# Order of issue in a fused retention and SwiGLU kernel: the later jobs' transposes two products behind a slot, their loads three

## The chip, the cores and the metric

The kernel runs on one NeuronCore of one Trainium2 chip. The metric is the device time of one execution in microseconds (us), as the median of three executions. A trace of one further execution gives the times of the single instructions; its span of 1141.5 us begins at the first instruction and ends with the last.

The engines of the core work side by side, each through its own instructions in the order in which the program wrote them: TensorE (PE in the profile) multiplies matrices, VectorE (DVE) and ScalarE (ACT) work on elements, GpSimd (POOL) does a little, and SyncE (SP) issues nearly all transfers between main memory (DRAM) and on-chip memory. "SPq" is SP's row of transfers. One row of issues serves the loads of queries, keys and values, the loads of weights and the stores of results.

## What is computed

```python
# retention, parallel form: 8 batches, 8 heads, 576 positions, 64 channels
scores = q @ k.T / sqrt(64)
ret    = scores * D            # D[i, j] = gamma_h ** (i - j) for i >= j, else 0
x      = (ret @ v)             # put together to 4608 tokens x 512 channels
# feed-forward with RMS norm and SwiGLU, 512 -> 1536 -> 512
xn  = x / sqrt(mean(x * x) + 1e-6) * rms_g
out = (silu(xn @ w_gate) * (xn @ w_val)) @ w_out
```

Queries, keys and values come as 32-bit floats. The weights come as 64-bit floats, and the kernel turns them into 32-bit floats itself: it loads both halves of each number as 32-bit words and takes sign, exponent and mantissa apart and together again with integer and float operations on VectorE and ScalarE.

## The kernel before

**Jobs.** Retention is cut into jobs of two heads each. Jobs 0 to 7 (batch 0 and a third of batch 1) are done at the start. Jobs 8 to 11 ("later jobs", the rest of batch 1) are done while the feed-forward of the first 768 tokens is already running. A job needs a load (`load_qk` and `load_kv`: 13 transfers), a turn (`prepare`: two transposes of 32 x 32 blocks on VectorE, and a scaling of the values on ScalarE) and a slot (`slot`: scores, states and sums of this job, and the values of the job before). The raw queries and keys have one buffer each, so a load waits in SP's row until the turn of the job before has read them.

```python
def load_qk(j):                       # 4 transfers for q, 4 for k; "raw" has one buffer
    ...
            t = raw.tile([P, S // SQ, SQ], F32, tag=nm + "raw", ...)
            ...
                    nc.sync.dma_start(out=t[...], in_=rows[i])            # L156
def load_kv(j):                       # 2 for k, 2 for v, 1 for the tail of v
    ...                                                                   # L224, L229
def prepare(j):                       # the turn
    for nm in ("q", "k"):
        ...
        nc.vector.transpose(out=t[:, t0:], in_=d.pop(nm + "raw")...)      # L272
    scale_v(j)                        # ACT, L285
def slot(j, rest=True):
    if rest and j > 0:
        values(j - 1)                 # PE, two PSUM banks av
    if j < len(jobs):
        scores(j)                     # PE
        states(j)                     # PE, one PSUM bank last
    ...
        weigh(j)                      # DVE
    if rest and j > 0:
        carried(j - 1)                # PE, then DVE empties av
    ...
        sums(j)                       # DVE, empties last
def prepare_next(j): prepare(j + 1)   # if there is such a job
def load_next(j): load_qk(j + 2); load_kv(j + 2)
def following(j):
    prepare_next(j)
    load_next(j)
```

**Chunks of weights.** There are 18 chunks of 1 MB as loaded: 0 to 11 for `w_gate` and `w_val`, 12 to 17 for `w_out`. Each is loaded into one of four spare places in buffers that aren't used yet. A place is free again when the last operation on the words of the chunk in it is done. The last six chunks use the places 1, 2, 3, 2, 3, 3, so that chunk 16 waits for 14 and chunk 17 for 16. The place 3 lies in the buffer of `w_gate`, the others in that of `w_out`.

```python
LATER = (1, 2, 3, 2, 3, 3)
def load_chunk(i, queue): ...
    queue.dma_start(out=dst, in_=src[rws, cols]...)      # L857
    there_at[i] = now + 3 if now else 0                  # not before 3 products from here
def exponent(i): ...                                     # DVE L874, then 3 x ACT L890 (act)
def mantissa(i):
    nc.vector.tensor_scalar(...);  yield                 # L901
    nc.vector.scalar_tensor_tensor(...);  yield          # L906, frees nothing yet
    act(chunk=i)                                         # the rest of the ACT operations
    nc.vector.scalar_tensor_tensor(...)                  # L911, last use of the words
    waits_at[spare(i)] = None                            # the place is free
def rounding():
    for i in range(len(chunks)):
        ...            # exponent(i), where it isn't done yet and the words may be there
                yield from mantissa(i)
                load_chunks(i + 5 if i else 0, nc.sync)
                yield
        ...            # exponent(i + 1) before or after that, where the words may be there
        join(i)                                          # L919
        yield
```

**The loop in which both meet.** The first 768 tokens go up through `w_gate` and `w_val` in 48 products, numbered by `now`. One product is 8 matmuls of 128 x 128 by 128 x 384 in the trace, and fills one of five PSUM banks that the whole kernel shares in rotation. Its result goes through `Silu` on ACT (L660) or is multiplied into that on DVE (L658), and that frees the bank. After each product come, in this order, what `later` has for this number, and two steps of the rounding.

```python
steps = rounding()
LATER_AT = (29, 33, 37, 41, 45)
def later(step):
    if step == LATER_AT[0] - 8:
        following(2 * NHP - 1)                 # turn 8, load 9
    elif step in LATER_AT:
        j = 2 * NHP + LATER_AT.index(step)
        if j < LATER_JOBS:                     # jobs 8 to 11
            slot(j, rest=(j > 2 * NHP))
            if j + 1 < LATER_JOBS:
                following(j)                   # turn j + 1, load j + 2
        else:
            values(j - 1)
            carried(j - 1)
...
for m, g in [(m, g) for g in range(NG) for m in range(2)]:
    for u in range(2):
        weights_to(4 * g + 2 * m + 1)
        for i, _ in enumerate(up_plain(u, m, g)):          # PE L652, then L660 or L658
            later(now)
            now += 1
            ...
            weights(2)
            act(1)
            if u and m and g == NG - 1:                    # products 44 to 47
                weights_to(len(chunks))
                next(made, None)                           # L690: blocks of w_out combined
            ...
```

After it the same tokens go down through `w_out` (`across(1)`, `across(0)`, PE L726), and then come ten rounds of 384 tokens each (PE L595 and L726) with the other jobs between them.

Of the kernel before, what the change touches and what calls it, by code (L numbers as in the profile page):

```python
# [22 lines left out]
def _decay_tables(H, D):  # L23

    pairs = _gamma(H).reshape(H // 2, 2).T
    rows = np.repeat(pairs, D, axis=0)
    pos = np.arange(L)
    p = np.concatenate([pos, pos])  # L30
    gq = rows[:, :, None] ** (pos + L) / np.sqrt(D)
    t = pairs.T[None] ** -p[:, None, None], rows**L, gq, np.roll(gq, D, axis=0)
    return [np.ascontiguousarray(x).astype(np.float32) for x in t]


def _causal_table():

    return np.ascontiguousarray(np.tile(np.triu(np.ones((L, L), np.float32)), (2, 1)))
# [3 lines left out]
def kernel(  # L42
# [15 lines left out]
    NHP = H // 2  # L58
# [29 lines left out]
    def bank(name):  # L88
        return banks.tile([P, 512], F32, tag="b", name=name)
# [46 lines left out]
    LATER_JOBS = 3 * NHP  # L136
# [9 lines left out]
    def load_qk(j):  # L146
        b, hp, c0, _ = jobs[j]
        for nm, src in (("q", q), ("k", k)):

            t = raw.tile([P, S // SQ, SQ], F32, tag=nm + "raw", name=f"{nm}raw_{j}")  # L150
            for e in range(2):
                rows = src[b, 2 * hp + e, c0 * L :]
                rows = rows.rearrange("(t b) (i a) -> i b t a", b=SQ, a=SQ)
                for i in range(D // SQ):
                    r = e * D + i * SQ
                    nc.sync.dma_start(out=t[r : r + SQ, c0 * L // SQ :], in_=rows[i])  # L156
            st[j][nm + "raw"] = t
# [58 lines left out]
    def load_kv(j):  # L216

        b, hp, *_ = jobs[j]
        i0, _ = tiles_of(j)
        for nm, src, bufs in (("k", k, 4), ("v", v, 3)):  # L220
            t = raw.tile([P, NFULL, 2, D], F32, tag=nm, name=f"{nm}_{j}", bufs=bufs)
            for e in range(2):
                rows = src[b, 2 * hp + e, i0 * P : NFULL * P]
                nc.sync.dma_start(  # L224
                    out=t[:, i0:, e], in_=rows.rearrange("(c p) d -> p c d", p=P)
                )
            st[j][nm] = t
        t = st[j]["vt"] = raw.tile([L, 2, D], F32, tag="vt", name=f"vt_{j}", bufs=3)
        nc.sync.dma_start(  # L229
            out=t, in_=v[b, 2 * hp : 2 * hp + 2, NFULL * P :].rearrange("e p d -> p e d")  # L230
        )
# [34 lines left out]
    def prepare(j):  # L266

        d = st[j]
        for nm in ("q", "k"):
            t = att.tile([P, S], F32, tag=nm + "T", name=f"{nm}T_{j}")  # L270
            t0 = jobs[j][2] * L
            nc.vector.transpose(  # L272
                out=t[:, t0:], in_=d.pop(nm + "raw")[:, t0 // SQ :].rearrange("p t a -> p (t a)")
            )
            d[nm + "T"] = t
        scale_v(j)
# [183 lines left out]
    def prepare_next(j):  # L460
        if j + 1 < len(jobs):
            prepare(j + 1)

    def load_next(j):
        if j + 2 < len(jobs):
            load_qk(j + 2)
            load_kv(j + 2)
# [4 lines that stand above are left out]
# [388 lines left out]
    def load_chunks(n, queue=nc.scalar):  # L860

        nonlocal n_loads
        while n_loads < min(n, len(chunks)) and waits_at.get(spare(n_loads)) is None:
            load_chunk(n_loads, queue)
            n_loads += 1
# [91 lines left out]
            yield  # L957

    steps = rounding()
    LATER_AT = (29, 33, 37, 41, 45)  # L960

    def weights(n):

# [13 lines left out]
    def start():  # L977

        nonlocal now
        h_of[0] = ffn.tile([P, NF, U], F32, tag="h", name="h_0")  # L980
        tables = list(zip((causal, gv, gc, gq, gx), (_causal_table(), *_decay_tables(H, D))))

        def table(i, queue):
            t, values_ = tables[i]
            src = nc.inline_tensor(values_, name=t.tensor.name + "_table")
            queue.dma_start(out=t, in_=src.ap())

        make_identity(nc, ident)
        nc.scalar.activation(out=tick, in_=mhalf[:1], func=AF.Silu)
        nc.vector.memset(ones, 1.0)  # L990
        warm = bank("warm")
        for _ in range(6):
            nc.tensor.matmul(warm[:, :P], lhsT=ones, rhs=ones, start=True, stop=True)
        first_places.update(find_places())
        load_chunks(1)
        for i in (1, 0, 2):
            table(i, nc.scalar)
        weights(3)
        for j in range(2 * NHP):
            load_first(j, {0: range(2), 1: range(2, H)}.get(j))  # L1000
            if j == 1:
                table(3, nc.sync)
            load_chunks((1, 1, 1, 1, 2, 2, 2, 3)[j], nc.sync)
        table(4, nc.sync)
        nc.sync.dma_start(out=rms_g, in_=moe_rms_g.rearrange("(c p) -> p c", p=P))
        load_chunks(4, nc.sync)
        turn(0)
        scale_v(0)
        act(3)
        squares = []  # L1010

        def later(step):

            if step == LATER_AT[0] - 8:
                following(2 * NHP - 1)
            elif step in LATER_AT:
                j = 2 * NHP + LATER_AT.index(step)
                if j < LATER_JOBS:
                    slot(j, rest=(j > 2 * NHP))
                    if j + 1 < LATER_JOBS:  # L1020
                        following(j)
                else:
                    values(j - 1)
                    carried(j - 1)

        for j in range(2 * NHP):
            slot(j)
            if j + 1 < 2 * NHP:
                turn(j + 1)
            if squares:  # L1030
                gather(*squares.pop())
            for i in ((1,), (2,), (3,), (4, 5), (6,), (7,), (), ())[j]:
                scale_v(i)
            if j:
                u, c = divmod(j - 1, NHP)
                squares.append((u, c, square(u, c)))
            act(1)
            if j == 5:
                norm_1(0)
            elif j == 6:  # L1040
                norm_2(0)
            weights((2, 0, 0, 1, 1, 1, 1, 0)[j])
            if j == 4:
                gather(*squares.pop())
            elif j == 5:
                diagonals(0)
            act(1)
        gather(*squares.pop())
        load_qk(2 * NHP)
        load_kv(2 * NHP)  # L1050
        made = combine_out()
        now = 0
# [3 lines that stand above are left out]
                for i, _ in enumerate(up_plain(u, m, g)):  # L1056
                    later(now)
                    now += 1
                    if not (u or m or g):
                        if i == 0:  # L1060
                            values(2 * NHP - 1)
                            carried(2 * NHP - 1)
                            gather(1, NHP - 1, square(1, NHP - 1))
                        elif i == 1:
                            norm_1(1)
                        elif i == 2:
                            diagonals(1)
                        elif i == 3:
                            norm_2(1)
                    weights(2)  # L1070
                    act(1)
                    if u and m and g == NG - 1:
                        weights_to(len(chunks))
                        next(made, None)
                    if i == 1:
                        weights_to(4 * g + 2 * m + 2)
        for _ in made:
            pass
        for blk, t in first_blocks.items():
            keep(blk, t)  # L1080
        rest = across(1)
        next(rest)
        following(LATER_JOBS - 1)
        for i, _ in enumerate(rest):
            if i == 1:
                norm_0(2)
                differences(0)
            elif i == 2:
                norm_1(2)
                diagonals(2)  # L1090
            elif i == 4:
                norm_2(2)
        rest = across(0)
        next(rest)
        combine(1)
        slot(LATER_JOBS, rest=False)
        following(LATER_JOBS)
        for _ in rest:
            pass
        combine(0)  # L1100
        slot(LATER_JOBS + 1)
        load_next(LATER_JOBS + 1)
        turns.append(LATER_JOBS + 1)
# [18 lines left out]
    with tc.manual_schedule():  # L1122
# [4 lines left out]
        for u in range(2, NU):  # L1127
# [11 lines left out]
            for i, _ in enumerate(rest):  # L1139
                if i == 0 and turns:  # L1140
                    prepare_next(turns.pop())
                if i == 2:
                    behind(u, 6)
                    at, n = SLOTS[u % 3]
# [33 lines left out]
```

## Time and profile before

| | |
|---|---|
| median of three executions | 1145.0 us (1144.41 to 1145.81) |
| execution with the trace | span 1141.5 us, mean granted TensorE clock 0.994 |
| busy share of the span | PE 98%, DVE 64%, ACT 23%, POOL 3% |
| the 48 products (L652) | first one at 47.4 us, last one at 191.6 us |
| loads of weight chunks (L857) | first 0.9 us (ACT's row), last 167.7 us (SP's row) |

The page of a profile gives totals over the whole span. For a change that moves a few instructions within a stretch of some 80 us, four other views are of more use: the list of waits (who stood still, for whom, how long in all, how often and the longest), the timeline of one engine (start, length, engine, line, operation), the chain that ended last, and the table of stretches (busy time of each engine, granted clock, DMA share and GB/s). A line such as L857 is one of kernel.py, printed above.

### The profile page before, as it was taken

How to read it: one execution, taken by the hardware profiler on the slowest of the kernel's cores; microseconds unless marked ns; L12 is line 12 of the kernel's file. 1: busy time of each engine (PE TensorE's matmuls, PEld its weight loads, DVE VectorE, ACT ScalarE, POOL GpSimd, SP SyncE). 2: the span in 40 equal slices, each digit the busy share in tenths (PEclk: the TensorE clock that was granted, in tenths of full speed). 3: DMA queues.
4: the chain of work that ended last, by engine and by line, in shares of the span. 5: the costliest groups of instructions: out<-in, count | busy, mean ns of one | idle time of the engine just before them, and what ended most of it. 6: DMA issues, size and time to landing. Idle time of an engine off the chain costs nothing.

```text
span 1141.5 us, 24777 instructions
## 1 busy us (share of the span) xinstructions
PE 1116.9 (98%) x10454; PEld 1041.7 (91%) x10454; DVE 733.0 (64%) x1452; ACT 258.0 (23%) x508; POOL 39.9 (3%) x68
## 2 busy tenths in 40 slices
PE   7899998999999999999999999999999999999998
PEld 6555655999999999999999999999999999999998
DVE  5888968746685685375767676466677566446352
ACT  5566532002211211211221121121121220120210
POOL 0100000380000000000000000000000000000000
PEclk8999999999999999999999999999999999999999
DMA  8744466335464465053454455305437503303304
GB/s 211 218 143 142 120 162 216 64 68 127 112 133 86 127 147 156 1 113 96 103 126 61 118 145 120 115 29 122 113 84 142 142 22 96 127 1 99 123 1 112
DMA packets 307040, 126.73 MB, mean 111 GB/s; under 512 B 284528, under 2 KB 289904, under 8 KB 306928
## 3 DMA queue, kind: packets, MB, share of 16 engines
q1 hardware_dynamic: 302640, 123.66, 42.8%
q8 instruction: 82, 1.34, 0.5%
q10 hardware_dynamic: 4288, 1.48, 0.5%
q14 instruction: 30, 0.25, 0.1%
HBM read 110.14 MB, written 14.94 MB: 110 GB/s over the span
## 4 chain that ended last, share of the span: by engine, by line
PE 89%; DVE 6%; DMA 1%; issue 1%; SPq 1%; ACT 1%; POOL 0%; DVEq 0%; POOLq 0%; ACTq 0%
PE w L595 13%; PE x L595 13%; PE z L595 13%; PE xo L726 8%; PE wo L726 8%; PE zo L726 8%; PE up L652 8%; PE y L595 6%; PE yo L726 4%; PE av L390 2%; PE s L307 1%; PE av L412 1%; PE s L329 1%; DVE sum L366 1%; DVE x L435 1%
## 5 line engine op out<-in xcount | busy, mean ns | idle before, releaser
L619 ACT COPY m<-x 128x384 f32<-128x384 f32 x60 | 28.7, 478 | 337.9 <-PE x L595 337.9
L726 PE MATMUL xo<-h,w_out 128*128 128x192 f32 x528 | 90.3, 328 | 0.0
L595 PE MATMUL w<-sums,w_val 128*128 128x192 f32 x480 | 88.6, 328 | 0.4
L595 PE MATMUL x<-x,w_val 128*128 128x192 f32 x480 | 88.8, 328 | 0.0
L595 PE MATMUL x<-x,w_gate 128*128 128x192 f32 x480 | 88.5, 328 | 0.0
L595 PE MATMUL w<-sums,w_gate 128*128 128x192 f32 x480 | 87.9, 326 | 0.0
L595 PE MATMUL z<-x,w_gate 128*128 128x192 f32 x480 | 87.8, 326 | 0.0
L595 PE MATMUL z<-x,w_val 128*128 128x192 f32 x480 | 87.8, 326 | 0.0
L726 PEld LDWEIGHTS xo<-h,w_out 128*128 128x128 f32 x528 | 85.9, 190 | 0.6
L726 PE MATMUL wo<-h,w_out 128*128 128x192 f32 x504 | 85.6, 326 | 0.4 <-DVE c_last L774 0.4
L602 DVE TENSOR_TENSOR u<-m,y 128x384 f32<-128x384 f32 x60 | 33.2, 553 | 79.1 <-PE y L595 79.1
L726 PEld LDWEIGHTS wo<-h,w_out 128*128 128x128 f32 x504 | 82.5, 190 | 0.7 <-DVE c_last L774 0.7
L595 PEld LDWEIGHTS w<-sums,w_val 128*128 128x128 f32 x480 | 79.2, 190 | 2.7 <-DVE c L602 2.7
L595 PEld LDWEIGHTS x<-x,w_val 128*128 128x128 f32 x480 | 79.2, 190 | 0.6
L595 PEld LDWEIGHTS x<-x,w_gate 128*128 128x128 f32 x480 | 79.3, 190 | 0.5
L595 PEld LDWEIGHTS z<-x,w_gate 128*128 128x128 f32 x480 | 79.7, 190 | 0.0
L595 PEld LDWEIGHTS z<-x,w_val 128*128 128x128 f32 x480 | 79.7, 190 | 0.0
L595 PEld LDWEIGHTS w<-sums,w_gate 128*128 128x128 f32 x480 | 79.5, 190 | 0.1
L602 DVE TENSOR_TENSOR h<-u,w 128x384 f32<-128x384 f32 x60 | 33.0, 551 | 69.5 <-PE w L595 69.5
L652 PE MATMUL up<-x,w_val 128*128 128x384 f32 x192 | 65.0, 497 | 5.6 <-DVE h L658 5.6
L614 ACT ACTIVATE h<-h 128x384 f32<-128x384 f32 x90 | 47.0, 523 | 88.7 <-DVE h L602 88.7
L652 PE MATMUL up<-x,w_gate 128*128 128x384 f32 x192 | 63.8, 489 | 2.0 <-DVE r L504 1.0
(189 smaller groups left out, 1774.6 us busy)
## 6 DMA issues: line engine op xcount, KB each, us to landing
w_out<-w_blocks SPq DMA_DIRECT2D x70, 768.0 KB, 4.9
out_dram<-o SPq DMA_DIRECT2D x364, 24.0 KB, 1.6
qraw<-in_q_dram SPq DMA_DIRECT2D x96, 72.0 KB, 2.6
kraw<-in_k_dram SPq DMA_DIRECT2D x96, 72.0 KB, 2.8
k<-in_k_dram SPq DMA_DIRECT2D x48, 128.0 KB, 2.8
v<-in_v_dram SPq DMA_DIRECT2D x48, 128.0 KB, 3.0
w_out<-in_moe_w_gate_dram SPq DMA_DIRECT2D x5, 1024.0 KB, 5.3
w_out<-in_moe_w_val_dram SPq DMA_DIRECT2D x3, 1024.0 KB, 5.2
```

The costliest lines, as they stand in the source:

```text
L307: nc.tensor.matmul(s[side(odd), e, i * L : i * L + L], lhsT=d["kT"][side(e), c * L : c * L + L], rhs=d["qT"][side(e), c * L : c * L + L], ...
L329: nc.tensor.matmul(o[side(e)], lhsT=d["k"][side(odd), i, e], rhs=d["v"][side(odd), i, e], start=True, stop=True,)
L366: nc.vector.scalar_tensor_tensor(out=d["sum"][c], in0=d["sum"][c - 1], scalar=gc[:, hp : hp + 1], in1=part, op0=ALU.mult, op1=ALU.add,)
L390: mm = nc.tensor.matmul(av[odd][column(j, odd, e), i * L : i * L + L], lhsT=d["v"][side(odd), i, e] if c < NC - 1 else d["vt"][:, e], rhs= ...
L412: mm = nc.tensor.matmul(av[odd][column(j, odd, e), i * L : i * L + L], lhsT=d["sum"][c - 1][side(e)], rhs=d["qT"][side(e), c * L : c * L + L],
L435: nc.vector.tensor_tensor(out=x[to, first - c0 // L :: 2], in0=av[odd][at, i * L : (i + n) * L].rearrange("p (c k) -> p c k", k=L), in1=g. ...
L595: nc.tensor.matmul(ps[:, i * HU : i * HU + HU], lhsT=w_up[m][:, 2 * blk + c, cut], rhs=t_of[u][blk][:, c], start=(start and i == c == 0), ...
L602: nc.vector.tensor_tensor(out=o, in0=a, in1=pairs_of(ps), op=ALU.add)
L614: nc.scalar.activation(out=o, in_=c, func=AF.Silu)
L619: nc.scalar.copy(out=s1, in_=pairs_of(x_))
L652: nc.tensor.matmul(ps[:, :U], lhsT=w_up[m][:, 4 * half + c, i * P : i * P + P], rhs=x_of[u][:, c], start=(c == 0), stop=(c == NHP - 1),)
L726: nc.tensor.matmul(ps[:, i * HU : i * HU + HU], lhsT=a[:, c, i * P : i * P + P], rhs=rhs[:, c], start=(start and i == c == 0), stop=False, ...
```

## The change

Slots, turns and loads of the later jobs are given other places among the 48 products. Slots come one product later. The turn of the next job no longer follows its slot directly but two products later, and the load of the job after that one more product later. In SP's row chunks of weights whose loads are written in between so stand ahead of these loads.

```diff
-    LATER_AT = (29, 33, 37, 41, 45)
+    LATER_AT = (30, 34, 38, 42, 46)
@@ def later(step):
-            if step == LATER_AT[0] - 8:
-                following(2 * NHP - 1)
-            elif step in LATER_AT:
+            for i, at in enumerate((LATER_AT[0] - 9,) + LATER_AT[:-2]):
+                if step == at + 2:
+                    prepare_next(2 * NHP - 1 + i)
+                elif step == at + 3:
+                    load_next(2 * NHP - 1 + i)
+            if step in LATER_AT:
                 j = 2 * NHP + LATER_AT.index(step)
                 if j < LATER_JOBS:
                     slot(j, rest=(j > 2 * NHP))
-                    if j + 1 < LATER_JOBS:
-                        following(j)
                 else:
                     values(j - 1)
                     carried(j - 1)
```

| after product | before | after the change |
|---|---|---|
| turn 8, load 9 | 21, 21 | 23, 24 |
| slot 8, turn 9, load 10 | 29, 29, 29 | 30, 32, 33 |
| slot 9, turn 10, load 11 | 33, 33, 33 | 34, 36, 37 |
| slot 10, turn 11, load 12 | 37, 37, 37 | 38, 40, 41 |
| slot 11 | 41 | 42 |
| values and carried part of job 11 | 45 | 46 |

No operation is added or taken away.

## The prediction

> **What bounds the kernel now.** I read the page first, then the list of waits, then the timelines of DVE and SP around the one wait that counts.
>
> ```profile
> span 1141.5 us, 24777 instructions
> PE 1116.9 (98%) x10454; PEld 1041.7 (91%) x10454; DVE 733.0 (64%) x1452; ACT 258.0 (23%) x508; POOL 39.9 (3%) x68
> ```
>
> PE is busy in 98% of the span, so a change of order can give back only idle time of PE. The list of waits says where PE stood still in the stretch that the change touches, and what stood behind it:
>
> ```profile
> DVE w_gate L874 <- DMA w_gate<-in_moe_w_out_dram: 10.2, 1, 10.2
> ...
> PE up L652 <- DVE h L658: 5.6, 1, 5.6
> ```
>
> PE waited once, 5.6 us, for a product to be read out of its bank (L658). DVE waited once, 10.2 us, for a chunk of weights. The timeline of DVE (start, length, engine, line) shows that they are one event:
>
> ```profile
> 156.75 0.75 DVE L342 SCALAR_TENSOR_TENSOR ret<-s,causal 128x256 f32<-128x256 f32 x2
> ...
> 160.00 0.57 DVE L272 STREAM_TRANSPOSE qT<-qraw 128x384 f32<-128x384 f32 x1
> 160.49 0.54 DVE L272 STREAM_TRANSPOSE kT<-kraw 128x384 f32<-128x384 f32 x1
> 160.95 1.18 DVE L911 SCALAR_TENSOR_TENSOR w_gate<-w_gate 128x1024 uint32<-128x1024 uint32 x1
> 162.17 1.23 DVE L919 SCALAR_TENSOR_TENSOR w_out<-w_out,w_gate 128x1024 f32<-128x1024 f32 x1
> 163.48 0.56 DVE L658 TENSOR_TENSOR h<-h,up 128x384 f32<-128x384 f32 x1
> 174.26 0.69 DVE L874 TENSOR_SCALAR w_gate<-w_gate 128x1024 uint32<-128x1024 uint32 x1 [10.22 <-DMA w_gate<-in_moe_w_out_dram]
> 174.87 0.69 DVE L901 TENSOR_SCALAR w_out<-w_gate 128x1024 uint32<-128x1024 uint32 x1
> 175.47 0.55 DVE L658 TENSOR_TENSOR h<-h,up 128x384 f32<-128x384 f32 x1
> ```
>
> L874 at 174.26 is the exponent of chunk 17. Behind it in DVE's row stands L658 of product 41, whose bank product 43 needs: five banks in rotation, and from 41 on they go to product 41, the two of slot 11's values, its `last`, product 42, and then to 43. PE resumes at 176.07. Why did chunk 17 come so late? SP's timeline:
>
> ```profile
> 160.60 1.96 SPq L156 DMA_DIRECT2D qraw<-in_q_dram  x4
> 162.65 2.06 SPq L156 DMA_DIRECT2D kraw<-in_k_dram  x4
> 164.76 1.05 SPq L224 DMA_DIRECT2D k<-in_k_dram  x2
> 165.92 0.99 SPq L224 DMA_DIRECT2D v<-in_v_dram  x2
> 167.02 0.61 SPq L229 DMA_DIRECT2D vt<-in_v_dram  x1
> 167.72 0.54 SPq L857 DMA_DIRECT2D w_gate<-in_moe_w_out_dram  x1
> ```
>
> Its place was free at 160.95 + 1.18 = 162.13, when L911 of chunk 16 ended. But load 12 stands ahead of it, starts when turn 11 has read the raw queries, and takes 7 us to issue. The chunk goes at 167.72 and lands at 174.2, 6.5 us after. One more line, from the table of stretches (busy times, then granted clock, DMA share, GB/s):
>
> ```profile
> 177.00:178.00 1.00, 1.00 (x3) 0.54 (x2) 0.95 (x4) 0.97 (x2) 0.00 (x0) 0.50 0.00 0
> ```
>
> After the stop PE runs at half its clock. The 8 matmuls of product 43 take 4.40 us on PE's timeline, those of 42 took 2.85: another 1.55 us. **The whole event costs 5.61 + 1.55 = 7.2 us.**
>
> **What the Trainium skill says.** "TensorE: Matmul & The Clock Gate", section "What's actually happening": the clock falls to half after an idle window of about 3.4 us and comes back after as long a busy one. The trace agrees: 5.6 us of idling, then 0.50 from about 175.5 to 178.9. So a stop well under 3.4 us should cost only itself. "DMA: Bandwidth & Descriptors", section "Anatomy of one DMA": "any semaphore wait happens on the issuing sequencer before dispatch". So a load whose buffer isn't free holds up all behind it; the chunk above, ready at 162.1 and gone at 167.7, shows it. "Perfetto Trace Analysis", section "Tensor Engine Instruction", has ACT and DVE as strict FIFO, PE with a little reordering; L658 at 175.47, whose product was there by about 166, shows it for DVE.
>
> **The change part by part.** From the code I listed what is written after each product. Loads of chunks 13, 14, 15, 16, 17 are written in the two rounding steps after products 22, 25, 30, 32, 37, and the change doesn't move them. It moves the loads of the jobs:
>
> - before: 12, load 9, 13, 14, load 10, 15, 16, load 11, load 12, 17
> - after: 12, 13, load 9, 14, 15, 16, load 10, load 11, 17, load 12
>
> So chunk 17 passes load 12, but load 11 now stands directly ahead of it. It won't go at once when its place is free.
>
> *PE.* A product is 2.63 us (four take 10.52, from 142.93 to 153.45), slot 8 0.98 us (129.75 to 130.73), a full slot 1.68 (141.25 to 142.93). Product 29 ends at 129.75 in both. After: product 36 ends at 129.75 + 7 x 2.63 + 0.98 + 1.68 = 150.8, product 38 at 156.1, slot 10 at 157.8, products 40, 41, 42 at 163.0, 165.7, 168.3, slot 11 at 170.0, product 43 at 172.6.
>
> *Chunk 16.* DVE work up to its load is the same as before (slot 8, turn 9, chunks 13 and 14), so it still goes at about 142.5, now with load 10 behind it. The one before took 8.3 us to land beside a load; I take that again: 150.8.
>
> *Turn 10 and load 11.* DVE has the exponent of 16 at about 150.9 (0.6), the join of 15 (1.2), then turn 10 from 152.7, with the queries read at 153.2. A load of 13 transfers took 8.0, 7.5 and 7.0 us to issue (133.56 to 141.55, 147.18 to 154.63, 160.60 to 167.63): 7.3 gives 160.5. The place of chunk 17 is free before that: behind turn 10 come 0.6 + 1.2 of mantissa and L911 with its ACT work, about 158. **Chunk 17 goes at 160.5** instead of 167.7. Landings of `w_out` chunks in the trace: 4.8, 5.5, 5.7, 5.9, 8.3, 6.5. I take 5.8, as load 11 is nearly through and nothing large is behind: it lands at 166.3, 8 us earlier.
>
> *DVE from there.* It has slot 10 (3.2 us) to about 161, L658 of product 40 to 163.7, turn 11 to 164.7, then waits some 1.6 us for the chunk instead of 10.2. Exponent and first mantissa to 167.4, L658 of 41 to 167.9, so product 43's bank is free well before 170. Three ACT operations of 1.15 from 166.9 end at 170.3; L911 to 171.5; L658 of product 42 at about 172.1. With slot 11 a product later, the rotation is 41, 42, values, values, `last`, 43, 44: product 44 needs 42's bank, at 172.6. It fits by half a microsecond, less than I can vouch for.
>
> *Behind.* DVE keeps that lag: slot 11 3.2, join 1.2, six L658 of 0.47, four L690 of 1.75, carried part of job 11 1.1, then L710 1.35 end near 189; `zo` of the first `across`, which reads L710's result, would begin 3.9 us after 184.6, at 188.5. Before, L710 ended at 195.9 and `zo` began at 196.13, as close. I put 0.3 to 0.5 us here.
>
> *Sum.* Back 7.2; given up again 0.3 to 0.5 at `zo` and on average 0.5 at product 44. Net 6.3. The 950 us behind are PE work with no dependence on this, and move up as a block. 1145.0 - 6.3 = 1138.7.
>
> **The rivals.** *The wait moves.* Load 11 still blocks the row; a landing of 8.3 instead of 5.8 puts L658 of 42 at 174.6 and stops product 44 for 2 us, at full clock afterwards. For it: the landing of chunk 16. Time 1140 to 1141. *A full gain:* all margins hold, also the 0.26 and 0.32 us PE waits nearby go: 1137.2. *Turns come too late:* a turn has two products (5.3 us) ahead of its slot, a load three (7.9) ahead of its turn while its issue alone takes 7.3; if values of job 11 came late at ACT, slots would stop PE and DVE would become the bound. Against it: load 11 is through at 160.5, its last transfer lands 2.3 later, slot 11 comes at 168.3. It would make 1143 to 1148. *Hidden anyway:* it isn't, since PE has no slack behind.
>
> **Range and chances.** Full gain and moved wait with run-to-run spread (0.7 us each way) give 1137.0 to 1141.0. 2% is 22.9 us, three times what the event costs, so faster by 2% is out of reach; slower by 2% would need a new stop of over 20 us.
>
> **What would show it.** In the profile after: the chunk load of SP (L857, last) near 160.5 and ahead of load 12; DVE's wait for it 1 to 3 us instead of 10.2; no granted clock of 0.50 between 165 and 192; PE's wait for L658 gone or under 2 us, and if there, ahead of product 44; product 47 ending near 185. Wrong, if load 11's issue starts much later than 153, if chunk 17 lands after 169, or if a slot waits for a transpose or a scaled value.

## The result, and the profile after

The changed kernel takes 1136.39 us (median of four executions, 1135.36 to 1138.52) where the kernel before took 1144.7 beside it: a ratio of 0.9928, with a 95% interval of 0.9911 to 0.9946. The prediction was 1138.7 with a range of 1137.0 to 1141.0, so the gain came out larger than the range allowed.

The page of the traced execution, its span and busy shares:

```profile
span 1135.3 us, 24783 instructions
PE 1116.6 (98%) x10454; PEld 1042.3 (92%) x10454; DVE 732.7 (65%) x1452; ACT 258.6 (23%) x508; POOL 40.9 (4%) x68
```

Work is the same on every engine. What changed is waiting. The list of waits of PE between 60 and 215 us, that is nearly all of the 48 products and the first part of the way down, is now

```profile
PE up L652 <- DVE x L564: 0.7, 1, 0.7
PE av L412 <- POOL tick L401: 0.3, 1, 0.3
```

Both were there before. The 5.6 us for L658 are gone, and so is a wait of 0.3 for L660 ahead of product 38 (more on that one below). No granted clock of one half is left between the products. SP's timeline shows load 11, then chunk 17, then load 12:

```profile
154.52 1.90 SPq L156 DMA_DIRECT2D qraw<-in_q_dram  x4
156.51 1.95 SPq L156 DMA_DIRECT2D kraw<-in_k_dram  x4
158.51 1.01 SPq L224 DMA_DIRECT2D k<-in_k_dram  x2
159.63 0.95 SPq L224 DMA_DIRECT2D v<-in_v_dram  x2
160.69 1.60 SPq L229 DMA_DIRECT2D vt<-in_v_dram  x1
162.39 0.54 SPq L857 DMA_DIRECT2D w_gate<-in_moe_w_out_dram  x1
165.99 1.95 SPq L156 DMA_DIRECT2D qraw<-in_q_dram  x4
```

and DVE's timeline the short wait for the chunk and the results of products 41 and 42 behind it:

```profile
165.89 0.54 DVE L272 STREAM_TRANSPOSE kT<-kraw 128x384 f32<-128x384 f32 x1
167.64 0.69 DVE L874 TENSOR_SCALAR w_gate<-w_gate 128x1024 uint32<-128x1024 uint32 x1 [1.21 <-DMA w_gate<-in_moe_w_out_dram]
...
168.85 0.55 DVE L658 TENSOR_TENSOR h<-h,up 128x384 f32<-128x384 f32 x1
...
171.91 1.23 DVE L911 SCALAR_TENSOR_TENSOR w_gate<-w_gate 128x1024 uint32<-128x1024 uint32 x1 [1.38 <-ACT w_gate L890]
173.06 0.55 DVE L658 TENSOR_TENSOR h<-h,up 128x384 f32<-128x384 f32 x1
```

The wait of DVE is 1.21 us instead of 10.22, because the transpose work of turn 11 and slot 10 now lies ahead of it and the chunk comes earlier. L658 of product 42 ends at 173.6, and PE starts product 44 near 174.3 without stopping.

**One measure for all runs.** The start of the kernel differs from execution to execution: the first product of `w_val` (product 8) begins between 72.8 and 74.9 us in the eleven traces of this study, in kernels that are the same up to there. So I measure the stretch on PE from the start of product 8 to the first matmul of `xo` in the way down, read from PE's timeline. Before it takes 192.24 - 72.90 = 119.34 us, after 186.29 - 74.36 = 111.93. **The stretch gives 7.41 us.** PE's timeline before, and then after the change:

```profile
72.90 20.80 PE L652 MATMUL up<-x,w_val 128*128 128x384 f32 x64
...
167.62 2.85 PE L652 MATMUL up<-x,w_val 128*128 128x384 f32 x8
176.07 9.56 PE L652 MATMUL up<-x,w_val 128*128 128x384 f32 x24 [5.61 <-DVE h L658]
...
192.24 4.06 PE L726 MATMUL xo<-w_val,w_out 128*128 128x192 f32 x24
```
```profile
74.36 20.80 PE L652 MATMUL up<-x,w_val 128*128 128x384 f32 x64
...
171.66 10.59 PE L652 MATMUL up<-x,w_val 128*128 128x384 f32 x32
...
186.29 4.06 PE L726 MATMUL xo<-w_val,w_out 128*128 128x192 f32 x24
```

From the start of the first of four products to the first matmul behind them it is 185.56 - 167.62 = 17.94 us with the stop and 182.17 - 171.66 = 10.51 us without. So the event alone costs 7.43 us: 5.61 of stop, 1.55 of slow clock, and some 0.27 because a stop also breaks the overlap of one product with the next (one product alone shows 2.85 us, but products in a row start 2.63 us apart). The small wait for L660 has no part in the 7.41: slot 10 takes 0.29 us less without it (1.70 for 1.99), and slot 9 0.28 us more (1.96 for 1.68).

| kernel | stretch, us | median beside before, us | ratio (95%) |
|---|---|---|---|
| before | 119.34 | | 1 |
| the change | 111.93 | 1136.39 : 1144.7 | 0.9928 (0.9911 to 0.9946) |
| e1, the change again | 111.93 | 1136.85 : 1144.09 | 0.9940 (0.9926 to 0.9953) |
| e2, load 12 alone moved | 111.92 | 1135.48 : 1144.09 | 0.9925 (0.9909 to 0.9940) |
| e3, slots alone moved | 113.95 | 1138.33 : 1144.09 | 0.9950 (0.9936 to 0.9965) |
| e4, last third undone | 120.71 | 1145.11 : 1144.09 | 1.0011 (1.0004 to 1.0017) |
| e5, chunk 17 from ACT's row | 111.95 | 1135.59 : 1143.69 | 0.9928 (0.9913 to 0.9942) |
| e6, chunk 17 inside load 12 | 113.64 | 1137.75 : 1143.69 | 0.9945 (0.9931 to 0.9960) |
| e7, first use written later | 111.92, then 4.8 lost at `zo` | 1140.03 : 1143.69 | 0.9964 (0.9949 to 0.9978) |
| e8, slots, and load 10 later | 117.62 | 1141.3 : 1143.69 | 0.9978 (0.9969 to 0.9988) |
| e9, turns and loads alone | 113.45 | 1139.27 : 1143.69 | 0.9957 (0.9943 to 0.9971) |

The differences of the medians follow the stretches to within 1.5 us; the intervals are as wide. Where less than that matters, the stretch decides.

### The profile page after: what moved, and what is told of

Its sections match the earlier page's. It is cut to its first block, busy times and chain, and to the rows that moved or that the text cites. A ratio compares the mean times of both kernels' runs of the same rounds, so it can differ in the third digit from the quotient of the medians.

```text
span 1135.3 us, 24783 instructions
## 1 busy us (share of the span) xinstructions
PE 1116.6 (98%) x10454; PEld 1042.3 (92%) x10454; DVE 732.7 (65%) x1452; ACT 258.6 (23%) x508; POOL 40.9 (4%) x68
## 4 chain that ended last, share of the span: by engine, by line
PE 96%; DVE 1%; DMA 1%; issue 1%; ACT 1%; SPq 0%; POOL 0%; POOLq 0%; ACTq 0%
PE x L595 14%; PE w L595 14%; PE z L595 14%; PE up L652 11%; PE xo L726 8%; PE wo L726 8%; PE zo L726 8%; PE y L595 7%; PE yo L726 4%; PE av L390 2%; PE av L412 2%; PE s L307 2%; PE s L329 1%; PE ms L513 1%; DMA first_sums<-in_v_dram 0%
```

## The experiments

The theory: chunk 17 was held up by what stands ahead of it in SP's row, its first use then held up DVE's row, and results behind that held up PE. The rivals: the room that later turns and slots give DVE is what counts; memory bandwidth is what counts; the change gives something outside of the stretch.

**e1: the change again,** unchanged.

> The changed kernel once more, to size its gain. Traces so far: from the end of product 29 to the first matmul of the down part the kernel before took 62.5 us and the changed one 55.1, so the stretch gave 7.4 (5.6 of stop, 1.55 of half clock, 0.26 of a small wait). The medians differ by 8.3. If the stretch is all there is (theory: the row of SP), the gain over five rounds is 7.4, and what is over comes from the start, whose length differs from run to run. Rival: the change gives something elsewhere too, and the gain is again above 8.

The stretch is again 111.93 us, and the ratio 0.9940. The medians differ by 7.2, not 8.3. Nothing outside of the stretch is needed to account for it. The traces say the same: from the first matmul of `xo` to the end of the span it is 949.3 us before, 949.0 after the change and 949.3 in e1.

**e2: only load 12 behind chunk 17,** in the kernel before.

```diff
             elif step in LATER_AT: ...
-                    if j + 1 < LATER_JOBS:
-                        following(j)
+                    if j + 1 < LATER_JOBS:
+                        prepare_next(j)
+                        if j < LATER_JOBS - 2:
+                            load_next(j)
+            elif step == LATER_AT[2] + 1:
+                load_next(LATER_JOBS - 2)
```

> The kernel before with one move only: the load of job 12 is written one product later, so that chunk 17 stands ahead of it. Slots and turns stay. Theory of the row: chunk 17 goes when its place is free, at 162.2, lands near 168, DVE waits about 4 us for it instead of 10.2, PE does not stop at all, the gain is the whole 7.4. Rival (later turns and slots give DVE room, the loads are by the way): gain under 2.

Chunk 17 went at 163.21, or 162.2 after the later start is taken off, DVE waited 3.7 us for it, and PE didn't stop for a result of DVE. Its small wait of before is still there:

```profile
PE up L652 <- ACT w_val L660: 0.3, 1, 0.3
```

One load written one product later gives all that the change gives: slots, turns and the other three loads needn't move.

**e3: only the slots one product later,** turn and load still right behind each.

```diff
-    LATER_AT = (29, 33, 37, 41, 45)
+    LATER_AT = (30, 34, 38, 42, 46)
-            if step == LATER_AT[0] - 8:
+            if step == LATER_AT[0] - 9:
```

> The kernel before with slots 8 to 11 one product later and turn and load still right behind each slot. That alone puts chunk 17 between load 11 and load 12 in the row of SP. Theory of the row: chunk 17 goes when its place is free, about 159 to 162, no stop of PE, gain 7.4, so two products more for the turns and three for the loads add nothing. Rival (it is the distance of turns and loads that counts): a stop of some us remains, gain 2 to 5.

The stop for chunk 17 is gone, as its load again passes load 12, but another one is there. The waits of PE and of DVE:

```profile
PE up L652 <- ACT h L660: 2.1, 1, 2.1
...
DVE w_gate L874 <- DMA w_out<-in_moe_w_out_dram: 4.5, 1, 4.5
```

This is chunk 15. It still stood behind load 10, which came later with its slot, and went at 144.09 instead of 141.65 (1.2 of that is the later start of this execution). DVE waited for it, an ACT operation of that chunk waited for DVE, and a result of PE (L660) stood behind that in ACT's row. The later issue explains 1.3 of DVE's 4.5 us. The rest fits the slot's own move: in the kernel before, DVE's work for slot 9 and turn 10 (143.3 to 147.6) stands ahead of this chunk's exponent and fills the time, and with the slot one product later it stands behind. I had looked only at chunk 17 and expected the whole 7.4; the stretch gives 5.4.

**e4: the last third of the change undone:** slot 10, turn 11 and load 12 again after product 37.

```diff
-    LATER_AT = (30, 34, 38, 42, 46)
+    LATER_AT = (30, 34, 37, 42, 46)
-            for i, at in enumerate((LATER_AT[0] - 9,) + LATER_AT[:-2]):
+            for i, at in enumerate((LATER_AT[0] - 9,) + LATER_AT[:2]):
...
                     slot(j, rest=(j > 2 * NHP))
+                    if j == LATER_JOBS - 2:
+                        following(j)
```

> The changed kernel with slot 10, turn 11 and load 12 put back behind product 37; everything else stays changed. Chunk 17 then stands behind load 11 and load 12, both late. Theory of the row: load 11 goes from 154 to 162, load 12 to 169, chunk 17 near 169.5, landing near 176; PE stops 6 to 8 us and falls to half clock; the whole gain is lost, 1144 to 1147. Rival (later turns and slots): most of the moves are still there, so half of the gain or more stays, under 1141.

SP's timeline gives chunk 17 at 169.27. PE's timeline shows the stop and what comes after:

```profile
177.31 13.57 PE L652 MATMUL up<-x,w_val 128*128 128x384 f32 x32 [5.68 <-DVE h L658]
```

Four products take 13.57 us where they take 10.59 at full clock. The whole gain is lost with two thirds of the moves still in place. The rival of "more room for DVE" falls. But SP's row isn't all of this delay. The place of chunk 17 came free only at 166.9, when L911 of chunk 16 ended: that had waited 4.6 us for ACT, and ACT had waited 5.4 us for the values of load 11, behind which turn 11 now stands directly. Load 12 held the chunk up for the last 2.4 us.

**e5: chunk 17 issued from ACT's row,** nothing else.

```diff
-                    load_chunks(i + 5 if i else 0, nc.sync)
+                    load_chunks(i + 5 if i else 0, nc.scalar if n_loads == 17 else nc.sync)
```

> The kernel before with one change: the transfer of chunk 17 is issued from ACT instead of SP; no order is changed. Theory of the row: ACT has no load ahead of it, so the chunk goes at 162.2 when its place is free and lands near 168.5, PE does not stop, gain 7.4 less what ACT's own row loses by waiting from 159 to 162 (under 0.5). Rival (the memory side is the limit, the chunk shares the bandwidth with load 12 in any case): landing stays after 172, gain under 3.

ACT's timeline, then one line of DVE's:

```profile
162.21 0.40 ACTq L857 DMA_DIRECT2D w_gate<-in_moe_w_out_dram  x1
162.65 0.87 ACT L660 ACTIVATE w_val<-up 128x384 f32<-128x384 f32 x2 [3.60 <-DVE w_gate L911]
```
```profile
167.91 0.69 DVE L874 TENSOR_SCALAR w_gate<-w_gate 128x1024 uint32<-128x1024 uint32 x1 [3.82 <-DMA w_gate<-in_moe_w_out_dram]
```

The transfer waited 3.6 us in ACT's row for its place and went at 162.21, while load 12 was being issued by SP from 160.64 on. The stretch is 111.95 us. With both on the way at once the chunk was there for DVE at 167.9: memory bandwidth isn't what held it up. Load 12 took 9.5 us to issue here instead of 7.0, which cost PE nothing.

**e6: chunk 17 in the middle of load 12.**

```diff
-                        following(j)
+                        prepare_next(j)
+                        if j < LATER_JOBS - 2: load_next(j)
+                        else: load_qk(j + 2)
+            elif step == LATER_AT[2] + 1:
+                load_kv(LATER_JOBS)
```

> The kernel before with chunk 17 in the middle of load 12: the 8 transfers of queries and keys ahead of it, the 5 of keys by rows and values behind. It goes near 164.7 and lands near 170.5 to 171. Product 41's result is then read out near 172.2, so PE stops for 1.5 to 2.5 us. If the slow clock comes only after an idle stretch of some 3.4 us, that stop costs itself alone and the gain is 5 to 6 us, with no granted clock of 0.50 in the stretch; if any stop brings the half clock, 1.5 less: 3.5 to 4.5.

PE's timeline:

```profile
172.27 8.01 PE L652 MATMUL up<-x,w_val 128*128 128x384 f32 x24 [1.44 <-DVE h L658]
```

The chunk went at 165.17. PE stopped for 1.44 us, and the three products after it took 8.01 us, full clock. The stop is 4.2 us shorter than before, and the stretch 5.7 shorter: the rest is the slow clock that didn't come, as expected (the 3.4 us are those of the page that the prediction names).

**e7: only the first use of chunk 17 written later,** no transfer moved.

```diff
-        there_at[i] = now + 3 if now else 0
+        there_at[i] = now + (6 if i == 17 else 3) if now else 0
```

> The kernel before with no transfer moved: only the first DVE operation on chunk 17 (exponent) is written three products later, behind the results of products 41, 42 and 43. Chunk 17 still lands at 174. If what stops PE is the wait inside DVE's row, ahead of results that PE's banks need, PE does not stop and the gain is 7 or more with SP's row as it was. If chunk 17 itself is needed by then, the stop comes a little later and most of the 7 stays lost.

PE no longer stopped at product 43, although the chunk was issued at 169.48 (168.0 on the scale of the kernel before) and first used at 175.77. So it was the wait inside DVE's row that stopped PE. But DVE's own chain got late. Its timeline, then PE's (`issue` means that the profile shows nothing that PE waited for):

```profile
191.77 1.35 DVE L710 TENSOR_TENSOR t<-w_val 128x1152 f32<-128x1152 f32 x1
```
```profile
186.30 4.06 PE L726 MATMUL xo<-w_val,w_out 128*128 128x192 f32 x24
193.23 5.82 PE L726 MATMUL zo<-t,w_gate 128*128 128x192 f32 x24 [2.86 <-issue]
```

`zo` normally begins 3.90 us after `xo`; here it was 6.93, and it took 5.82 instead of 4.06 at half clock: 3.03 + 1.76 = 4.8 us given back. The late join and combination of `w_out` (L690) pushed L710, which `zo` reads: it ended at 193.12, and `zo` began 0.11 us later. Half of my expectation held; I hadn't followed the chunk past product 47.

**e8: the slots of e3, and load 10 behind chunks 15 and 16.** Turn 10 stays right behind slot 9, after product 34.

```diff
 (beside the lines of e3)
+            elif step == LATER_AT[0] + 3:
+                load_next(2 * NHP)
...
-                        following(j)
+                        prepare_next(j)
+                        if j > 2 * NHP:
+                            load_next(j)
```

> Slots one product later with turn and load right behind each, and one more move: load 10 is written after product 33, behind chunks 15 and 16. With the slots alone chunk 15 went only at 144.1, behind load 10, DVE waited 4.5 us for it, and PE 2.1 us for a result that ACT held up. If that chunk behind that load made the whole stop, it is gone here: chunk 15 goes near 139, the stretch takes 111.9 us as in the changed kernel, gain 7.4. If the slots' new place stops PE by itself, some 2 us stay lost.

Chunk 15 went at 137.57, and its stop was gone. But load 10 went at 142.75, and its turn came one product behind. Waits of PE, then ACT's timeline:

```profile
PE last L329 <- ACT w_val L660: 1.8, 1, 1.8
PE av L390 <- ACT h L660: 1.2, 1, 1.2
PE up L652 <- ACT w_val L660: 0.7, 1, 0.7
```
```profile
153.26 0.45 ACT L285 ACTIVATE v<-v,gv 128x192 f32<-128x192 f32 x1 [7.54 <-DMA v<-in_v_dram]
```

ACT waited 7.5 us for the values that the turn scales, with results of PE behind it. The stretch is 5.7 us longer than that of the change, an outcome that I hadn't named. A load that goes later needs its turn to go later too, as e4 shows as well; the change moves the turns by two products.

**e9: turns and loads as changed, slots as before.**

```diff
-    LATER_AT = (30, 34, 38, 42, 46)
+    LATER_AT = (29, 33, 37, 41, 45)
-            for i, at in enumerate((LATER_AT[0] - 9,) + LATER_AT[:-2]):
+            for i, at in enumerate((21, 30, 34, 38)):
```

> The changed kernel with the slots (and the last values) back at products 29, 33, 37, 41, 45; turns and loads stay where the change has them, after 23 and 24, 32 and 33, 36 and 37, 40 and 41. The order in SP's row is that of the changed kernel. Theory of the row: gain 7.4, stretch of 111.9 us, so the slots' move gives nothing. Rival (a turn one product ahead of its slot is too near): PE waits up to 1 us in slots 10 and 11, gain 6 to 7.

```profile
PE s L307 <- DVE kT L272: 1.6, 1, 1.6
```

The order of SP's row is that of the change, but a turn now lies one product ahead of its slot, and in slot 10 PE waited 1.6 us for a transpose. The stretch is 1.5 us longer than with the slots moved as well. The rival held here, with a longer wait than it named: with the turns moved, slots at their old places cost something. The distance alone isn't the reason. In e4 turn 10 lies one product ahead of slot 10 too, and PE didn't wait: there the transposes ended 80.6 us after the start of product 8, here 82.7 us after it, behind a wait of DVE of 1.95 us for ACT.

## Why the prediction was wrong

**What bounds, and why: right.** One event, and its chain (load 12 ahead of chunk 17, L874 ahead of L658, bank of product 41, PE). Its cost was a quarter of a microsecond too small: I had 7.2, from start to start it is 7.43, as the overlap with the next product is lost as well. The two small waits that I had put into the full gain gave nothing: the one of 0.26 us went, but slot 9 got as much longer, and the one of 0.32 us stayed. One reading was loose. The passage that I quoted on semaphore waits describes transfers that GpSimd issues; for SP's row it is the trace that shows such a wait, 5.9 us ahead of load 12. And this wait was over at 160.60. From 162.1, when the chunk's place was free, SP was busy issuing load 12.

**The new order and its times: right.** The traced execution begins product 8 1.46 us later than that of before; taken off, chunk 17 went at 160.9 (I had 160.5), was used at 166.2 (166.3), and L658 of product 42 ended at 172.15 (172.1). In e1 SP issued it at 160.93, with its product 8 0.42 later than before.

**The step that failed: "given up again 0.3 to 0.5 at `zo` and on average 0.5 at product 44".** Both terms measured nothing. At product 44 the half microsecond that I saw was enough: the bank was read out 0.7 us ahead of it, and neither trace of the change lists a wait there. At `zo` I had DVE keep its lag to the end. In the trace the lag is gone before that: ahead of the last two L690 DVE waits 0.53 us for PE (`av`, L412), and it begins to read out product 47 at 186.49, 0.2 us after `xo` has begun behind that product. So L710 ended at 188.63 + 1.35 = 189.98, `zo` began at 190.19, 3.90 us after `xo`, and no wait is listed. With the later start taken off that is 188.5 and 188.7, where I had 189 (my own terms add up to 188.8) and 188.5. I took margins that came out near zero for expected losses. As to the margins the rival of the full gain was the true case. Of the miss of 2.3 us, 0.9 is this and 0.2 the event's cost.

**The base.** I started from 1145.0, three executions. Over the 25 executions of the kernel before that ran beside e1 to e4 the median is 1144.09. Base less stretch is 1144.09 - 7.41 = 1136.7, between the 1136.39 and 1136.85 measured. So about 0.9 us more of the miss is the base, and what remains, 0.3, is inside the spread of a few executions. This part of the split is an estimate: beside the changed kernel itself the base was 1144.7, in four executions.

**The range.** I gave the full gain as 1137.2 and the spread as 0.7 each way, and then put the lower end at 1137.0. By those numbers it had to be 1136.5, still 0.1 above the measured time; the base's own error belonged in it as well.

**The rivals.** That the wait moves: not in the change, but e7 and e3 are this rival in other orders. That turns come too late: not in the change; in e9 PE waited for one (1.6 us), and in e8 and e4 a turn stood too close behind its load (ACT waited 7.5 and 5.4 us).

## What to carry to other kernels

In a row of issues that runs in order, look for what stands ahead of the transfer that ends last, and ask when this transfer could have gone without it: one load moved behind one chunk (e2) was worth as much as the whole rearrangement. The same holds on DVE and ACT: an operation that waits for a late transfer must not stand ahead of one that frees a bank PE needs (e3, e7, e8). When a sum of margins comes out near zero, it is a range of outcomes that begins at no loss at all, not a loss.

## What the runs showed of the hardware

The profile before shows a stop of PE that cost more than itself, as the clock fell to half (175.8 to 179.2 us in the trace, not 175.5 to 178.9 as the prediction has it). The runs show that how much more differs. "TensorE: Matmul & The Clock Gate", section "What's actually happening", names an idle window of about 3.4 us, free-running. Here stops of 1.4 (e6), 1.6 (e9) and 2.1 us (e3) brought no slow clock, the stop of 2.9 us in e7 brought 3.4 us of it (194.4 to 197.8 in the trace), and 5.6 to 5.7 us brought 3.4 us before but 6.8 in e4 (176.5 to 183.4), about 3 us lost instead of 1.55. In e8 three stops of 1.8, 1.2 and 0.7 us within some 6 us brought 3.4 us as well. So a stop needn't reach 3.4 us. In e4 PE resumed 0.8 us after the clock had fallen, before the change 0.25 us after. Where the free-running window begins may be what decides; no run here varied that alone.
